# Attention and a multiplicative ffn on one core: the planner's choices replaced by written-out orders for five engines

## The chip, the cores and the metric

The kernel runs on one core of one Trainium2 chip. The metric is the device time of one execution in microseconds; the time of a kernel is the median of its runs. Profiles come from one profiled execution each; its span runs from the first to the last instruction of the program.

## What is computed

```python
# q, k, v: 8 batches, 12 heads, 448 positions, 64 per head; x: 3584 tokens, d_model 768, d_ff 1024
q_n, k_n = rmsnorm(q, g_q), rmsnorm(k, g_k)
scores = scale * np.matmul(q_n, k_n.transpose(0, 1, 3, 2))
attn = np.exp(scores - max); attn = attn / attn.sum(-1)
x = np.matmul(attn, v)            # heads side by side: (3584, 768)
a, b = x @ w1, x @ w2
out = ((a * b) @ w3) @ w_out      # float32
```

## The kernel before

The 96 heads are worked in 24 quads of four heads, three quads to a batch. For each quad, q and k are loaded (`load_qk`), squared on ACT, summed on DVE, scaled to bf16 by DVE, and transposed, by TensorE for the first five quads (`do_turn`, L1163) and by a DMA on SP's queue for the others. The scores of a quad are seven units of two PSUM banks each (`do_score`, L716), and ACT's exp of each unit (L738) writes P. A value block (`start_pv`, L803 and L782) multiplies P with v and with ones for one quad or for two; ACT forms the reciprocal of the sums by Ln and Exp (L825, L826) and DVE multiplies it into xT (L845).

The product w3 @ w_out is formed once: each of eight blocks of 128 rows of w3 is loaded, turned by TensorE (`do_w3_turn`, L1185), copied to w3T, and used by one "w" pair of eight positions on w_out's four chunks. Then each batch has eight "f" pairs (`ffn1_pair`: for each two blocks of d_ff one with w1, whose sums are copied to a_sb by ACT or DVE, and one with w2, whose sums DVE multiplies with that copy into abT, L989), and each two batches have seven "o" pairs (`ffn2_pair`) that multiply abT with w34s and whose sums are copied to `half` (L369 on ACT, L375 on DVE) and stored. The last o tile is done apart (`do_last`, L1104).

A pair (`Pair`, `do_pass`, L908) has two PSUM banks. A pass is four matmuls on 64 by 64 tiles of TensorE, of 448 columns for f and 384 for w and o; f has 12 passes, w and o have 16. In the middle of a pair the two row halves change banks: `hand_over` puts an empty instruction on SP or POOL that waits for the last matmul of the first half, and the first matmul of the second half waits for it. Until `gap_at` no pass of the pair is planned.

All instructions are emitted by a `Planner` that runs its own clock over five engines with a duration for each job. Before the change, each of ACT, DVE, SP and POOL took, whenever it was free, the job that could start first, then the one with the lowest key; jobs with two possible engines went to the one that finished earlier; and TensorE's next step came from rules in `pe_try` with margins, limits and keys (`PAIRS`, `MARGINS`, `HUNGERS`, `STOCKS`, `AGAINST` and others). Whatever the planner chose is a fixed program on the chip: each engine runs its list in order and waits on semaphores. Weights, v and five of the quads' q and k are loaded through POOL's queue in the order of `POOL_ORDER`, at most eight transfers in flight; the others through SP's. Until 13.2 us of the planner's clock, TensorE fills free time with matmuls on a constant tile (`do_warm`, L1233), after sixteen longer ones at the start (L1360).

Of the kernel before, what the change touches and what calls it, by code (L numbers as in the profile page):

```python
# [23 lines left out]
DRAIN = 0.11  # L24
LAG = {"ACT": 0.11, "DVE": 0.09, "SP": 0.0, "POOL": 0.0}
# [3 lines left out]
BUSY = 75.0  # L29


class Job:
# [4 lines left out]
    def __init__(self, engine, took, key, emit, needs=(), done=None, moves=None):  # L37
        self.took = took if isinstance(took, dict) else {engine: took}
        self.key, self.emit, self.needs, self.done = key, emit, needs, done
        self.moves, self.any = moves, isinstance(took, dict)  # L40
# [5 lines left out]
class Planner:  # L46
# [3 lines left out]
    def __init__(self):  # L50
        self.free = {e: 0.0 for e in ("ACT", "DVE", "SP", "POOL", "PE")}
        self.jobs = []
# [5 lines left out]
    def add(self, *args, **kw):  # L58
        self.jobs.append(Job(*args, **kw))
# [37 lines left out]
    def commit(self, job, start, engine):  # L97
# [3 lines left out]
        self.jobs.remove(job)  # L101
# [28 lines left out]
    def run(self, pe_step, finished):  # L130

        stuck = 0
        while not finished() or self.jobs:
            best = None
            behind = {
                e: sum(
                    job.took[e]
                    for job in self.jobs
                    if e in job.took
                    and not job.any  # L140
                    and job.ready() <= max(self.free[e], self.now) + 0.3
                )
                for e in ("ACT", "DVE")
            }
            for e in ("ACT", "DVE", "SP", "POOL"):
                mine = []
                for job in self.jobs:
                    if e not in job.took:
                        continue
                    ready = job.ready()  # L150
                    if job.moves is not None:
                        ready = max(ready, self.lane_free(e))
                    if ready < INF:
                        at = max(ready, self.free[e], self.now)
                        if job.any and any(
                            max(ready, self.free[x], self.now) + job.took[x] + behind[x]
                            < at + job.took[e] + behind[e]
                            for x in job.took
                        ):
                            continue  # L160
                        mine.append((at, job.key, job))
                if not mine:
                    continue
                first = min(m[0] for m in mine)
                start, _, job = min(
                    (m for m in mine if m[0] <= first + 1e-9), key=lambda m: m[1]
                )
# [1285 lines left out]
```

## Time and profile before

| | |
|---|---|
| Median of 3 runs | 350.99 us (350.04 to 351.31) |
| Span of the profiled execution | 348.0 us |
| PE busy | 342.3 us, 98% |
| ACT, DVE, POOL busy | 260.8, 206.7, 76.9 us |
| Chain that ended last | PE 98%, of which L908 68%, L803 13%, L716 9% |
| Granted TensorE clock | 0.998 over the span |
| DMA | 55.11 MB, 158 GB/s on average |

The execution's own time is its span and some 3 us around it. PE busy is the union of the matmuls' own durations; since a matmul of 0.35 us is followed by the next pass after 0.19 us, a busy PE need not be a PE that starts a pass as soon as it can. For that the start of one pass is to be set against the start of the next. A letter q behind an engine's name (POOLq, SPq) is its queue of instructions that only issue or wait.

### The profile page before, as it was taken

Reading aid. Unit: us, or ns where it says so; the run is one execution under the profiler, and the core shown is the slowest. Engines: PE = TensorE matmul, PEld = TensorE weight load, DVE = VectorE, ACT = ScalarE, POOL = GpSimd, SP = SyncE. Lnnn points to the kernel's source line nnn. Section 1 sums busy time; section 2 is a strip of 40 time slices with the busy share of each in tenths; the row PEclk is TensorE's granted clock in tenths of the full one; section 3 lists DMA queues with packets and bytes.
Section 4 is the critical chain, followed back from the end, with each engine's and each line's share of the span. In section 5 each row is a group of like instructions: output and inputs, shape, how many; then the busy total and the mean of one; then the engine's idle time right before and its main releaser. Section 6 shows DMA issues by size and latency. Waiting matters only on the chain.

```text
span 348.0 us, 16174 instructions
## 1 busy us (share of the span) xinstructions
PE 342.3 (98%) x7373; PEld 219.3 (63%) x7373; DVE 206.7 (59%) x296; ACT 260.8 (75%) x371; POOL 76.9 (22%) x134
## 2 busy tenths in 40 slices
PE   8999999999999999999999999999999999999995
PEld 4767756656775756566666575566665665666674
DVE  5369289898956687486567963865894313222100
ACT  4779989999997997998799797978987882222122
POOL 8556820302222301222022022212204000000000
PEclk9999999999999999999999999999999999999999
DMA  8999999499995969948898699477898051000055
GB/s 197 206 312 204 241 299 268 89 202 199 208 187 174 92 156 188 260 107 154 148 246 161 169 165 259 116 131 186 197 185 105 7 133 53 4 2 2 4 166 155
DMA packets 68488, 55.11 MB, mean 158 GB/s; under 512 B 45060, under 2 KB 62372, under 8 KB 68420
## 3 DMA queue, kind: packets, MB, share of 16 engines
q1 hardware_dynamic: 49440, 35.33, 43.0%
q0 software_dynamic: 18048, 16.92, 29.6%
q10 hardware_dynamic: 932, 1.84, 1.4%
q8 instruction: 57, 0.93, 1.1%
q14 instruction: 11, 0.09, 0.1%
HBM read 46.66 MB, written 11.01 MB: 166 GB/s over the span
## 4 chain that ended last, share of the span: by engine, by line
PE 98%; ACT 1%; DVE 0%; issue 0%
PE ps_all L908 68%; PE ps_all L803 13%; PE ps_all L716 9%; PE ps_all L782 2%; PE ps_all L1360 2%; PE ps_all L1163 1%; PE ps_all L1185 1%; PE ps_all L1104 1%; PE ps_all L1233 1%; ACT P L738 0%; DVE abT L989 0%; ACT qk_sb L369 0%; DVE warm_t L1343 0%; PE ps_all L1373 0%
## 5 line engine op out<-in xcount | busy, mean ns | idle before, releaser
L738 ACT ACTIVATE P<-ps_all 128x896 bf16<-128x896 f32 x114 | 99.5, 916 | 11.7 <-PE ps_all L716 10.8
L424 POOL DMA_DIRECT2D v_sb<-in_v_dram x96 | 57.3, 611 | 184.1 <-PE ps_all L716 120.3
L908 PE MATMUL ps_all<-xT,w2s 64*64 64x448 bf16 x1536 | 88.5, 349 | 0.0
L908 PE MATMUL ps_all<-xT,w1s 64*64 64x448 bf16 x1536 | 86.5, 349 | 0.0
L908 PE MATMUL ps_all<-w34s,abT 64*64 64x384 bf16 x1728 | 80.2, 323 | 0.4 <-DVE abT L989 0.4
L369 ACT ACTIVATE half<-ps_all 128x896 bf16<-128x896 f32 (+1 forms) x35 | 30.6, 874 | 48.5 <-PE ps_all L908 48.3
L908 PEld LDWEIGHTS <-abT 64*64 64x64 bf16 x1728 | 51.7, 107 | 20.3 <-issue 0.7
L908 PEld LDWEIGHTS <-w2s 64*64 64x64 bf16 x1536 | 46.5, 107 | 25.6
L908 PEld LDWEIGHTS <-w1s 64*64 64x64 bf16 x1536 | 46.0, 107 | 25.7 <-issue 0.4
L716 PE MATMUL ps_all<-qkT 64*64 64x448 bf16 x672 | 60.3, 351 | 0.0
L989 DVE TENSOR_TENSOR abT<-ps_all,half 128x896 bf16<-128x896 f32 x32 | 34.8, 1089 | 41.2 <-PE ps_all L908 41.1
L492 DVE TENSOR_REDUCE ssq<-sq 128x14 f32<-128x896 f32 (+1 forms) x50 | 51.2, 1041 | 12.5 <-ACT sq L487 12.2
L526 DVE TENSOR_TENSOR qks<-qk_sb,al 128x448 bf16<-128x448 f32 x96 | 54.6, 616 | 4.8 <-ACT al L504 4.7
L487 ACT ACTIVATE sq<-qk_sb 128x896 f32<-128x896 f32 (+1 forms) x50 | 45.1, 917 | 1.6 <-DMA qk_sb<-in_q_dram 1.3
L845 DVE TENSOR_TENSOR xT<-ps_all,r 128x448 bf16<-128x448 f32 x48 | 27.5, 618 | 25.6 <-ACT r L826 22.0
L716 PEld LDWEIGHTS <-qkT 64*64 64x64 bf16 x672 | 21.7, 106 | 13.2 <-issue 4.2
L908 PE MATMUL ps_all<-w_outs,w3T 64*64 64x384 bf16 x512 | 25.1, 324 | 0.1
L803 PE MATMUL ps_all<-P,v_sb 128*32 128x448 bf16 x456 | 25.0, 352 | 0.0
L738 ACT ACTIVATE w_outs<-ps_all 128x896 bf16<-128x896 f32 x24 | 21.4, 915 | 3.2 <-PE ps_all L716 3.0
L803 PEld LDWEIGHTS <-v_sb 128*32 128x32 bf16 x592 | 15.9, 97 | 12.2 <-issue 0.2
L738 ACT ACTIVATE Pr<-ps_all 128x896 bf16<-128x896 f32 x24 | 22.1, 920 | 0.6 <-PE ps_all L716 0.5
L375 DVE COPY half<-ps_all 128x768 f32<-128x768 f32 x13 | 12.4, 955 | 12.7 <-PE ps_all L908 12.7
(63 smaller groups left out, 210.9 us busy)
## 6 DMA issues: line engine op xcount, KB each, us to landing
out_dram<-half SPq DMA_DIRECT2D x48, 192.0 KB, 3.3
qk_sb<-in_q_dram SPq DMA_DIRECT2D x15, 448.0 KB, 6.3
qk_sb<-in_k_dram SPq DMA_DIRECT2D x15, 448.0 KB, 5.4
v_sb<-in_v_dram POOLq DMA_DIRECT2D x48, 64.0 KB, 4.0
v_sb<-in_v_dram POOLq DMA_DIRECT2D x48, 48.0 KB, 4.1
qk_sb<-in_q_dram POOLq DMA_DIRECT2D x5, 448.0 KB, 8.7
qk_sb<-in_k_dram POOLq DMA_DIRECT2D x5, 448.0 KB, 9.4
w3s<-in_moe_w_dram POOLq DMA_DIRECT2D x8, 256.0 KB, 6.8
```

The source lines that it names most:

```text
L369: nc.scalar.activation(out=out, in_=in_, func=AF.Copy, scale=1.0 if by is None else by)
L375: nc.vector.tensor_copy(out=out, in_=in_)
L424: nc.gpsimd.dma_start(out=v_bufs[i % 4][p0 : p0 + HP, g::2, 0 : j1 - j0].rearrange("p h j d -> p h (j d)"), in_=src[:, g::2, j0:j1].rearra ...
L487: nc.scalar.activation(out=out, in_=in_, func=AF.Square)
L492: nc.vector.tensor_reduce(out=s["ssq"][:, t, x0:x1], in_=s["sq", t][:, x0:x1], axis=AX, op=ADD)
L526: nc.vector.tensor_tensor(out=s["qks"][:, t, :, x], in0=src[:, t, x], in1=s["alpha"][:, t, x].unsqueeze(2).broadcast_to([NP, NJ, D]), op=MULT,
L716: nc.tensor.matmul(out=sc[HP * c : HP * c + HP, u, 0:S].rearrange("p (j s) -> p j s", j=NJ), lhsT=qkT[u * D : (u + 1) * D, 1, j, cols], rh ...
L738: lambda: nc.scalar.activation(out=dst, in_=sc[:, :, 0:S], func=AF.Exp),
L803: nc.tensor.matmul(out=ps_all[hd * HALF : (hd + 1) * HALF, z, 0:S], lhsT=value_weights(i, hd, j, kind), rhs=s["P"][:, hd, j, :] if j < NF ...
L845: lambda: nc.vector.tensor_tensor(out=xT[b][:, 2 * m + kind - 1, :], in0=ps, in1=s["r"], op=MULT),
L908: mm = nc.tensor.matmul(out=ps_all[64 * h : 64 * h + 64, p.bank + z, 0 : p.n], lhsT=lhsT[64 * r : 64 * r + 64, 64 * h : 64 * h + 64], rhs= ...
L989: nc.vector.tensor_tensor(out=abT[bp][:, f0 : f0 + 2, odd * S : (odd + 1) * S], in0=ps_all[:, z : z + 2, 0:S], in1=a_sb[b, f0], op=MULT,)
```

## The change

Five strings list what each engine does, in order: `PE_ORDER` (x: turn of a w3 block, t: turn of a quad's q or k, s: score unit, V and v: value block and its steps, w, f, o: passes of the pair with that number, L: last tile), `ACT_ORDER` and `DVE_ORDER` (s squares, r sums, a scales, c scaled q and k, T, x, w, f, o copies, e exps, n reciprocals, m and h products, g gains), `SP_ORDER` and `POOL_ORDER` (l, v, W loads, t transposes, O, Z stores, hand-overs not listed). The planner keeps its clock and takes the next name of each list as soon as its conditions hold; `follow` replaces `pe_try`. On POOL two blocks of w3 (`Ww0 Ww1`) now stand ahead of w_out's first chunk, and q and k of quad 1 ahead of its last; TensorE turns the two blocks first. `gap_at` lies 0.32 us behind the hand-over instead of 0.15; banks that have been free for `WHILE` = 0.3 us are preferred; constants of the planner's clock change. A job that fills a buffer of `half` now has its condition at the copy (`free_of`) and no longer at the pair's start.

```diff
+WHILE = 0.3
...
+PE_ORDER = (
+    "x0 x1 t*2 w0 s w0 s x2 s w0*2 w1*2 s w0*2 w1*2 s w1*2 w0 s w0 w1*2 w0 w1*2 s w2 w0 w2*3 w0 "
+    "w1 V1 v*2 w2*2 w0 w2*4 w1 w0 w1 w0 w2*2 w1 w0*2 w2 w1 w2 w1 x3 x4 t w2 w3*3 w4 w3*2 w4 w3*2 "
...
+    "f12*3 s f13*6 V2 v*8 f14 s f14*5 f15 s f15*2 f14 s f15 f14 f15 f14 s f15 f14 s f14*2 f15 s "
+    "f15*5 s*4 o3*6 o4*5 o3*2 o4*3 s o3*3 s o3*4 o4 o3 s o4*7 V2 v*8 s o5*5 o6 o5 o6 s o6 o5*2 o6 "
...
+ACT_ORDER = (
+    "s0q0 s0q1 s0k0 s0k1 a0q a0k T0q e0.0 e0.1 e0.2 e0.3 e0.4 e0.5 e0.6 n0 s1q0 s1k0 a1q w0 w1 "
...
+DVE_ORDER = (
+    "r0q0 r0q1 r0k0 r0k1 c0q0 gp c0q1 c0k0 c0k1 gs x0 T0k x1 x2 m0.1 m0.2 r1q0 r1k0 c1q0 c1q1 x3 "
...
+POOL_ORDER = (
+    "Ww0 Ww1 Wo0 Ww2 Wo1 Wo2 v0.3 v0.2 v0.1 v0.0 l1q0 l1k0 Wo3 Ww3 Ww4 l2q0 l2k0 Ww5 l3k0 Ww6 "
...
+    "v6.2 v8.2 v8.0 v6.3 v8.1 v9.0 v9.2 v9.3 v9.1 v10.1 v8.3 v11.1 v10.2 v10.0 v10.3 v11.0 v12.1 "
...
+    "v18.0 v19.1 v20.3 v18.3 v20.2 v21.3 v23.0 v20.0 v21.0 v20.1 v22.1 v21.1 v21.2 v23.2 v22.0 "
...
+                if self.done[e] == len(ORDERS[e]):
                     continue
...
+                job = self.jobs.get(ORDERS[e][self.done[e]])
+                if job is None:
+                    continue
+                ready = job.ready()
+                if job.moves is not None:
+                    ready = max(ready, self.lane_free(e))
+                at = max(ready, self.free[e], self.now)
+                if at < INF and (best is None or at < best[0]):
+                    best = (at, job, e)
...
-    POOL_ORDER = (
-        "o0 w0 w1 w2 o1 o2 v0 u0 o3 q1 w3 w4 q2 w5 v1 u1 a0 w6 w7 v2 u2 a1 u3 v3 q3 a2 b0 b1 q4 q5 b2".split()
-    )
...
-    FIRST = 3.5
+    FIRST = 2.9
...
-        p.gap_at = free[e] + 0.15
+        p.gap_at = free[e] + 0.32
...
+    def follow(t, step):
+        early, idle = idle_banks(t - WHILE), idle_banks(t)
+        idle = early + sorted((z for z in idle if z not in early), key=lambda z: bank_at[z])
+        two = adjacent(early)
+        two = adjacent(idle) if two is None else two
+        one = single(early or idle)
+        kind = step[0]
+        if kind == "s":
+            n = next_score[0]
+            i, g = divmod(n, NU)
+            if two is None or max(qkT_at[i]) + SEM > t:
+                return None
...
+            return do_score(t, two)
...
+        p = next((p for p in pairs if p.id == step), None)
+        if p is None:
+            p = next((p for p in waiting if p.id == step), None)
+            if p is None or two is None or p.ready() > t:
+                return None
+            waiting.remove(p)
+            start_pair(p, two)
+            return do_pass(p, t)
+        return do_pass(p, t) if p.ready() <= t else None
...
+    def pe_step(t):
+        if place[0] >= len(ORDER):
             return None
...
+        took = follow(t, ORDER[place[0]])
+        if took is not None:
+            place[0] += 1
+        elif t < WARM_TO and idle_banks(t):
             return do_warm(single(idle_banks(t)))
         return took
...
-            warm(1)
+            free["PE"] = max(free["PE"], plan.now + 0.35)
...
-        warm(WARM)
+        warm(WARM + 1)
```

## Rows read from the trace of the kernel before

**Rows 1.** The page, busy us (share of the span) and instructions of each engine

```profile
PE 342.3 (98%) x7373; PEld 219.3 (63%) x7373; DVE 206.7 (59%) x296; ACT 260.8 (75%) x371; POOL 76.9 (22%) x134
```

**Rows 2.** Waits of PE: who waited for whom, us in total, times, longest

```profile
PE ps_all L908 <- DVE abT L989: 0.4, 1, 0.4
```

**Rows 3.** The chain that ended last, in order of time: start us, us, what

```profile
18.16 2.46 PE ps_all L803 x48
...
168.22 3.41 PE ps_all L908 x84
...
215.48 0.69 PE ps_all L782 x24
216.17 3.52 PE ps_all L803 x72
...
222.46 2.27 PE ps_all L908 x48
...
289.29 52.05 PE ps_all L908 x1152
341.34 2.78 PE ps_all L1104 x64
```

**Rows 4.** Timeline, head: start, us, engine, line, out<-in, count [idle before <- releaser]

```profile
7.80 0.60 POOL L424 DMA_DIRECT2D v_sb<-in_v_dram  x1 [0.41 <-DMA w_outs<-in_moe_w_out_dram]
...
8.69 0.93 PE L1233 MATMUL ps_all<-warm_t 128*128 128x256 bf16 x7
...
9.10 0.59 POOL L424 DMA_DIRECT2D v_sb<-in_v_dram  x1 [0.70 <-DMA w3s<-in_moe_w_dram]
...
10.29 0.38 PE L1233 MATMUL ps_all<-warm_t 128*128 128x256 bf16 x2
...
11.05 0.57 PE L716 MATMUL ps_all<-qkT 64*64 64x448 bf16 x8
...
11.48 5.10 ACT L738 ACTIVATE P<-ps_all 128x896 bf16<-128x896 f32 x6 [1.59 <-PE ps_all L716]
...
12.80 0.97 PE L908 MATMUL ps_all<-w_outs,w3T 64*64 64x384 bf16 x12
...
13.56 0.73 POOL L384 DMA_DIRECT2D qk_sb<-in_k_dram  x1 [1.13 <-DMA w_outs<-in_moe_w_out_dram]
```

**Rows 5.** Timeline around the turns of w3 blocks 3 and 4

```profile
21.33 0.59 POOL L424 DMA_DIRECT2D v_sb<-in_v_dram  x1 [0.52 <-DMA qk_sb<-in_k_dram]
...
22.42 0.59 POOL L424 DMA_DIRECT2D v_sb<-in_v_dram  x1 [0.50 <-DMA w3s<-in_moe_w_dram]
...
23.92 1.32 PE L1185 MATMUL ps_all<-ident,w3s 128*128 128x128 bf16 x16
24.44 0.57 POOL L455 DMA_DIRECT2D w1s<-in_moe_w_dram  x1 [1.43 <-DMA w3s<-in_moe_w_dram]
24.47 0.60 PEld L1185 LDWEIGHTS <-w3s 128*128 128x128 bf16 x10 [0.21 <-issue]
```

**Rows 6.** Timeline at the end of batch 1, around 115 us

```profile
114.44 0.96 PE L716 MATMUL ps_all<-qkT 64*64 64x448 bf16 x12
114.67 1.09 DVE L989 TENSOR_TENSOR abT<-ps_all,half 128x896 bf16<-128x896 f32 x1 [0.23 <-PE ps_all L908]
...
115.81 1.33 PE L908 MATMUL ps_all<-w34s,abT 64*64 64x384 bf16 x28 [0.41 <-DVE abT L989]
```

**Rows 7.** Windows: stretch, then busy us (count) of PE, PEld, DVE, ACT, POOL; clock, DMA, GB/s

```profile
5.00:15.00 10.00, 9.88 (x141) 7.17 (x143) 6.86 (x14) 6.64 (x13) 5.77 (x9) 1.00 1.15 203
45.00:100.00 55.00, 55.00 (x1176) 35.76 (x1164) 48.16 (x70) 50.69 (x79) 11.32 (x20) 1.00 0.91 207
```

**Rows 8.** DVE's copies of f sums, forms kept apart: busy us, mean ns | idle before

```profile
L375 DVE CAST half<-ps_all 128x896 bf16<-128x896 f32 x11 | 12.0, 1090 | 11.1 <-PE ps_all L908 10.9
```

**Rows 9.** Timeline of PE's weight loads in the fill of the start

```profile
4.58 0.15 PEld L1360 LDWEIGHTS <-warm_t 128*128 128x128 bf16 x1 [0.28 <-issue]
5.01 0.15 PEld L1360 LDWEIGHTS <-warm_t 128*128 128x128 bf16 x1 [0.28 <-issue]
```

More of the change, by code (lines that the diff above doesn't have):

```diff
@@ L29, with unfold @@
 BUSY = 75.0
+PE_ORDER = (
[41 rows of a table added]
+)
+ACT_ORDER = (
[18 rows of a table added]
+)
+DVE_ORDER = (
[18 rows of a table added]
+)
+SP_ORDER = (
[9 rows of a table added]
+)
+POOL_ORDER = (
[8 rows of a table added]
+)
+def unfold(text):
+    return [
+        x.split("*")[0] for x in text.split() for _ in range(int((x + "*1").split("*")[1]))
+    ]
+ORDER = unfold(PE_ORDER)
+ORDERS = {
+    "ACT": ACT_ORDER.split(), "DVE": DVE_ORDER.split(),
+    "SP": SP_ORDER.split(), "POOL": POOL_ORDER.split(),
+}
 class Job:
@@ L100, in commit @@
         end += LAG[engine]
-        self.jobs.remove(job)
+        del self.jobs[ORDERS[engine][self.done[engine]]]
+        self.done[engine] += 1
         job.at = start
@@ L134, in run @@
             best = None
[L135 to L141, printed above, removed]
-                )
-                for e in ("ACT", "DVE")
-            }
-            for e in ("ACT", "DVE", "SP", "POOL"):
[L146 to L162, printed above, removed]
-                    continue
[L164 to L167, printed above, removed]
-                if best is None or start < best[0]:
-                    best = (start, job, e)
+            for e in ("ACT", "DVE", "SP", "POOL"):
+                if self.done[e] == len(ORDERS[e]):
+                    continue
+                job = self.jobs.get(ORDERS[e][self.done[e]])
[7 more added lines that the diff above has]
+                    best = (at, job, e)
             pe_at = max(self.free["PE"], self.now)
@@ L830, in done @@
                 s["r_at"] = e + SEM
-            add("ACT", 1.06, -1000.0, reciprocal, needs=[lambda: at], done=done)
+            add("n%d" % i, "ACT", 1.05, -1000.0, reciprocal, needs=[lambda: at, lambda: all_of(m_at[i - 2], 2) if i >= 2 else 0.0], done=done)
             return
@@ L861 @@
     running = [None]
+    made = {}
     class Pair:
@@ L1201, in do_w3_turn @@
         return took
-    def next_pair(t):
-        if len(pairs) >= (EARLY_PAIRS if w_at["w_out"][3] == INF else PAIRS[phase()]):
-            return None
-        return next((p for p in waiting if p.ready() <= t), None)
-    def any_turn(t, r, idle, n):
-        if not idle:
-            return None
-        if turns:
-            i, w = turns[0]
-            if scaled_at[i][w] <= r:
-                turns.pop(0)
-                return do_turn(t, i, w, single(idle))
-        ready = [fc for fc in w3_turns if w_at["w3"][fc] + SEM <= r]
-        if ready and (len(ready) >= n or ready[-1] == CF - 1):
-            if ready[0] - len(w34_at) < AHEAD_W3:
-                return do_w3_turn(t, w3_turns.pop(0), single(idle))
-        return None
@@ L1399, with weight @@
         seq = [0]
-        def weight(emit, moves, done):
-            add("POOL", 0.6, -100.0 + seq[0], emit, done=done, moves=moves)
-        for name in POOL_ORDER:
+        def weight(name, emit, moves, done):
+            add("W" + name, "POOL", 0.6, -100.0 + seq[0], emit, done=done, moves=moves)
+        for name in LOADS.split():
             what, x = name[0], int(name[1])
```

281 lines of the change are left out of this document (119 added, 162 removed), and 85 rows, old and new, of tables (ACT_ORDER, DVE_ORDER, PE_ORDER, POOL_ORDER).

## The prediction

> **What bounds the kernel now.** I read the busy row of the page first, then PE's waits, then the chain of work that ended last. PE is busy for 342.3 of 348.0 us [rows 1], and in the whole run its longest wait inside the work is one of 0.4 us, for a product of DVE [rows 2]. That leaves two questions: does a busy PE work at its rate, and how much of its time is not work. The chain answers the first. Twelve passes of 448 columns take 2.27 us (0.189 us each), 21 passes of 384 columns 3.41 us (0.1624 us each), and a double value block 0.69 + 3.52 = 4.21 us. The last 288 passes, with nothing but ffn work, take 52.05 us; 192 x 0.189 + 96 x 0.1624 = 51.9 us [rows 3]. So PE runs at its rate, at the full clock, and the work itself cannot shrink: the change removes no pass.
>
> Now the sum of the work, with the counts of the lists, which are those of the old kernel too: 768 f passes and 168 score units at 0.189 us (145.2 + 31.8), 432 o and 128 w passes at 0.1624 (70.2 + 20.8), eleven double value blocks at 4.21 (46.3), two single ones at 2.46 (4.9) [rows 3], 18 turn groups of about 0.42 (7.6), and the last tile 2.8 [rows 3]. Together 329.6 us. From the first turn (the warm-up fill that follows it starts at 8.69 [rows 4], 0.4 us after it) to the end of the last tile at 344.1 [rows 3] are some 335.7 us. So only about 6 us between them are no work. Of these, PE's changes between kinds of work (ffn passes, turns, value sums) take most: I count 54 such changes in the old order and 54 in the new list, kind for kind, so they stay. What order can win is the rest: 0.93 + 0.38 us of warm-up fill between the first turns, 0.29 us in the w passes at 12.80 (twelve matmuls in 0.97 us, where three passes span 0.68) [rows 4], 0.26 us in the turns of w3 blocks 3 and 4 (the two groups would span 1.06, two at 0.45 and 0.16 for the last matmul's own end, and span 1.32) [rows 5], and 0.8 us at 115 [rows 6]. That is 2.7 us, 0.8%. Anything over that must come from nowhere in this trace.
>
> **Head: blocks 0 and 1 of w3 ahead of w_out.** The POOL queue's waits show its landings, since an issue waits for the one eight places before: w_out chunk 0 by 7.80, w3 block 0 by 9.10, w_out chunk 1 by 13.56 [rows 4]. A block takes 1.3 us, a chunk 1.9. Put first, block 0 lands 1.9 - 1.3 = 0.6 us before chunk 0 did, at about 6.9 to 7.2, block 1 at 8.2 to 8.5, chunk 0 at 10.2 to 10.4. The list makes PE turn both blocks before the first turn of q, so that turn goes from 8.3 to about 8.8; its copy is ACT's and has room, since the first scores wait for the copy of k, which needs the second turn and has its place on DVE behind one w3 copy: it is done at about 10.7 in both kernels. First scores then at about 10.85 instead of 11.05 [rows 4]. The seven exps that follow (0.84 us apart, six in 5.10 us with the last one's own 0.92) end about 0.2 us earlier, and the first value block can start at about 17.5 instead of 18.1 [rows 3]. But the new list has 26 w passes ahead of it, the old order 28: 0.6 - 0.32 = some 0.27 us won. That is 0.27 of the 1.6 us that the head loses; the rest stays lost because PE is then held by ACT's exps and by w_out's chunks, and no longer fills.
>
> After that block both orders do 20 w passes and then blocks 3 and 4. The two loads of quad 1 now go ahead of w_out's chunk 3; the bytes are the same, so chunk 3 lands where k's load landed before, by 21.33 [rows 5]. The list needs it after eight w passes: 17.5 + 2.4 + 0.1 + 8 x 0.1624 = 21.3, just in time (0 to 0.2 us lost). Block 4 is the gate. In the old order its turn was not late for its load: the stop lies inside the turn of block 3, after six of its eight weight loads, and the profile puts it down to issue; block 4 had landed by 24.44 [rows 5], less the 0.3 us that an issue trails a landing. The new list comes to it earlier: value block done at 20.0, 20 w passes, block 3 from 23.4, block 4 wanted at 23.8. If it lands as before, at some 24.2, PE waits 0.4 us, turns it at 24.3 instead of 24.6 and has two w passes (0.32) less behind it: even. If the stop of 0.26 in block 3's turn comes again on top: +0.26. If block 4 lands a block's 1.3 us after block 3 (by 22.42), so before 23.8: -0.4. I take 0.0, from the row of the same bytes, and keep both ends. The Trainium skill (DMA: Bandwidth & Descriptors, the section on queues, rings and completion order) says that each of the sixteen engines takes its own ring in order, while the engines finish one transfer independently of each other; a strict queue would give the -0.4, rings drifting apart the 0.0, and the rows with block 4 two microseconds behind block 3 speak for the second.
>
> **The stop at 115.** At the end of batch 1 nothing is left for PE but three scores and an o pair that reads the product of the f pair just finished. DVE starts that product 0.23 us after the pair and takes 1.09 us; the o pair starts at 115.81, 1.56 us after the pair's last pass began (114.25, one pass before the score that shows at 114.44) [rows 6]. The new list has the same place: five f15 passes, four scores, then o3. The chain of 1.56 us stays; scores and the pass fill 0.189 x 5 = 0.945 us of it instead of 0.756. So the idle time falls from 0.80 to 0.61 us, if the fourth score finds banks; the banks of four scores in a row come free at ACT's 0.81 to 0.84 us each, so it may come too late and win little. Between -0.19 and 0: I take -0.1.
>
> **Hand-overs and banks.** A half pair's hand-over counts 0.32 us after its empty instruction instead of 0.15, so other passes are put between the halves; this costs nothing while other pairs are open (the new list mixes f and o passes, both with 64-row tiles, a change that costs nothing in the chain: f to o at 0.189, o to f at 0.162). Banks free for 0.3 us are preferred. In the profiled run hand-overs cost almost nothing, so the gain there is 0; but the three runs lie between 350.04 and 351.31, and late hand-overs are one cause that such a spread can have. I credit a third of the 0.95 us from median to lowest: -0.3, bounds 0 to -0.95.
>
> **Small edits.** The fill matmul that stood behind the product of the gains now stands with the others ahead of it; PE fills there anyway, so 0 (without that cover, one matmul of 0.2 us). The planner's new constants move its own clock alone: with the orders listed they still choose banks, fill and the engine of a hand-over, and cost nothing of themselves.
>
> **Copies moved.** Of the 24 f copies before the last two batches, ACT has 8 in the lists, before 13; DVE gets five more at 1.09 us, ACT loses five at 0.92, the exp's own size and time [rows 4, 8]. None is on the path that sets the end as long as DVE keeps up: from 45 to 100 it is busy for 48.16 of 55 us [rows 7] and gets about two there, 50.3 of 55. Cost 0, cover 4.7 us; what a loss of that cover costs is the second rival. Orders of SP and POOL: POOL's list puts some v pieces behind loads that wait for a later quad's buffer (v6.3 behind v8.2 and v8.0, v20.0 behind v23.0), and hand-over instructions stand in the same queues; each has several microseconds before its value block reads it. Cost 0 to +0.8, one more stop of the size at 115; I take 0.
>
> **Sum.** 0.0 - 0.1 - 0.3 + 0 = -0.4 us on the median of 350.99 (the profiled span is 348.0; some 3.0 us lie outside it and stay): **350.6 us**. The bounds add up to -0.4 - 0.19 - 0.95 = -1.5 and +0.26 + 0.2 + 0.8 = +1.3: 349.5 to 352.3. About 0.5%, or 1.75 us, is what a measurement of this kernel can tell from no change; the forecast lies inside.
>
> **Rivals.** First, everything order can win is won: no stop at 115, no wait about block 4, the head filled. For it: PE is the only bound and the loss is known place by place. Against: the list itself keeps f15, scores, o3 and keeps block 4 right behind block 3. 350.99 - 2.7 = 348.3, with one place left 348.8. Chance 0.15. Second, DVE becomes the bound: from 45 to 115 it gets f copies and keeps all products. For it: 92% busy with them by the sum above. It decides once DVE runs more than a product (1.09 us) late, since a pair's two banks then stay closed and PE stops as at 115, 0.6 to 0.8 us each; with four such places 2.4 to 3.2 us: 353.8. Against: the old trace has one wait of PE for DVE, at 115, and DVE was idle before that product [rows 2, 6]. Chance 0.09. Third, the clock. The rows show 1.00 for the granted clock from 5 to 15 us [rows 7], with turns between warm-up fill; weights for the 512-column fill were loaded 0.43 us apart at 4.58 and 5.01 [rows 9], at 1.2 GHz, where fill of 256 columns later took 0.11 each. If the clock fell as fill gives way to turns, a stretch like the first, 1.2 to 5.3 us, would run at half speed: 2.05 us lost, 353.0. Chance 0.03. The Trainium skill (TensorE: Matmul & The Clock Gate, Part 4 on transposes) says that transposes do not count as activity for the gate; by that rule the new head, with two more turn groups before the scores and less fill, is the place to look. Fourth, the lists turn out to give nearly the old timing everywhere: 351.0, chance 0.04. The forecast has the other 0.69.
>
> **How the numbers follow.** Faster by over 0.5% (below 349.24): the first rival and 0.01 of the forecast's edge, 0.16. Slower (above 352.74): second and third rival and 0.01, 0.13. The rest, 0.71. For 8 in 10 the range goes from 349.0, which takes in part of the first rival, to 352.4.
>
> **What would show it.** Right: first scores near 10.85, first value block near 17.5, the turn of block 4 near 24.3; three or four scores and then an idle PE of 0.6 us near 113 to 115, released by the product; 54 changes of kind; last tile ending 0 to 1 us earlier. Wrong: PE waiting on banks held by DVE between 60 and 110, a granted clock below 1.00 after 7 us, more than one wait over 0.3 us after 25 us, or no stop at all before o3.

## The result: 1.4% slower, and where the time went

The changed kernel takes 355.82 us (median of 4, 355.21 to 355.91) beside 351.15 us of the kernel before: a ratio of 1.0141, 95% interval 1.0113 to 1.0168, so 4.0 to 5.9 us more. The forecast was 350.6 us with a range of 349.0 to 352.4; the measured time lies above it. Every ratio, and the medians of E6 and E8, leave out slow executions (one each of E6 and E8). The profiled run took 355.91 us, its span is 354.1 us at a granted clock of 0.996, 6.1 us over the span of the kernel before.

This pair of profiles overstates the loss. In every execution for which both are on record the time is 1.73 to 1.86 us over the span; the "some 3 us around it" named ahead of the prediction came from setting a median beside the span of one execution. So the profiled execution of the kernel before stands for some 349.8 us, 1.3 us under its median, and the one of the changed kernel for its median.

The page of the changed kernel, busy row and the row of TensorE's code queue (packets, MB, share of the DMA engines):

```profile
PE 346.3 (98%) x7368; PEld 240.3 (68%) x7368; DVE 218.0 (62%) x307; ACT 252.1 (71%) x360; POOL 76.8 (22%) x134
...
q8 instruction: 57, 0.93, 1.1%
```

Beside [rows 1], PE is again busy for 98%: the busy row hides the loss, since a stop of 50 ns between pipelined matmuls doesn't show as idle. PEld rises from 219.3 to 240.3 us though it loads the same weights, at 107 ns for each of the passes' loads in both pages: fewer of them overlap. That doesn't measure the loss, for E7, which loses less than half as much, still has 238.7 us. DVE has its 11 us more and ACT its 9 us less, as the lists say.

The chain of the changed kernel (start us, us, what), its head, its last stretch and the last tile:

```profile
9.40 0.62 PE ps_all L1261 x8
10.02 0.39 PE ps_all L1239 x7
...
18.99 2.46 PE ps_all L871 x48
...
293.43 52.75 PE ps_all L981 x1152
346.17 2.78 PE ps_all L1180 x64
```

The single value block takes 2.46 us and the last tile 2.78 us, to the hundredth what [rows 3] shows. The last 288 ffn passes, the very same work, take 52.75 us instead of 52.05: 0.70 us of stops in a stretch where no load and no score is left. That is the pattern of the whole kernel. To see it everywhere I added up the work of the passes done (0.189, 0.1624 us and so on, as in the forecast) and compared the times at which both kernels had done the same amount ("lag" is the difference):

```
work done (us)   before at   changed at   lag    what lies between
     7             16.9        18.0       1.16   head: turns, first scores, first w_out passes
    30             41.2        42.3       1.03   turns of blocks 3 and 4 win 0.25
    34             45.3        47.6       2.27   43 to 46 us: +1.24
    95            107.7       110.1       2.43
   105            118.6       121.2       2.59   stop at the end of batch 1
   150            164.2       167.2       3.07
   210            224.9       228.5       3.55
   270            285.5       289.6       4.14
   328            343.9       348.8       4.84   from 118 us on: +2.3, in steps under 0.15
  end of span     348.0       354.1       6.1    tail: +1.27
```

**The head.** The timeline of the changed kernel (columns as in [rows 4]):

```profile
7.46 0.62 PE L1261 MATMUL ps_all<-ident,w3s 128*128 128x128 bf16 x8
...
9.40 0.62 PE L1261 MATMUL ps_all<-ident,w3s 128*128 128x128 bf16 x8 [0.45 <-DMA w3s<-in_moe_w_dram]
9.64 0.59 POOL L517 DMA_DIRECT2D v_sb<-in_v_dram  x1 [1.34 <-DMA w3s<-in_moe_w_dram]
...
11.52 0.73 POOL L477 DMA_DIRECT2D qk_sb<-in_q_dram  x1 [1.29 <-DMA w_outs<-in_moe_w_out_dram]
...
11.89 0.38 PE L801 MATMUL ps_all<-qkT 64*64 64x448 bf16 x4
```

PE stands before the turn of block 1 until 9.40, because the list wants that turn before the two turns of q and k, and block 1 lands at 9.35 (POOL's issue follows at 9.64); chunk 0 of w_out lands at 11.24. The first scores come at 11.89 instead of 11.05 [rows 4].

The clock in that stretch (columns as in [rows 7]):

```profile
5.00:15.00 10.00, 9.54 (x112) 5.57 (x114) 6.83 (x14) 5.57 (x11) 5.35 (x9) 1.00 1.13 198
```

**43 to 46 us.** PE's timeline, and the waits of its weight loads from 43 to 46 us (who for whom: us in total, times, longest):

```profile
42.91 0.83 PE L981 MATMUL ps_all<-w_outs,w3T 64*64 64x384 bf16 x14
44.14 0.51 PE L981 MATMUL ps_all<-w_outs,w3T 64*64 64x384 bf16 x6 [0.40 <-issue]
```

```profile
PEld L981 <- issue: 0.8, 1, 0.8
PEld L981 <- SPq L965: 0.5, 1, 0.5
```

The first is a hole of 0.59 us in the middle of a pass, with no semaphore to wait for; the second is the hand-over of pair w7 (line 965), whose two halves the list puts next to each other: 0.41 us between passes that need none. The value block behind them waits another 0.13 us longer than before for the last exp.

**From 118 us on.** Waits of PE's weight loads from 118 to 346 us, first the changed kernel, then the kernel before:

```profile
PEld L801 <- issue: 3.3, 11, 0.8
PEld L981 <- issue: 3.2, 14, 0.4
PEld L871 <- issue: 3.0, 8, 0.4
PEld L850 <- issue: 2.6, 8, 0.4
```

```profile
PEld L803 <- issue: 3.0, 8, 0.4
PEld L782 <- issue: 2.6, 8, 0.4
PEld L716 <- issue: 2.6, 7, 0.4
PEld L908 <- issue: 0.4, 1, 0.4
```

Passes (L981, before L908) were held up noticeably once and are now held up 14 times, scores (L801, before L716) 11 times instead of 7; value blocks are the same. The starts of passes and scores show it more sharply. Behind 118 us, 29 of them come over 30 ns later than the spacing of 0.189 or 0.1624 us asks for, each 41 to 43 ns after the release of a PSUM bank by an exp, a copy or a product (22 by ACT, 7 by DVE). One is the stop at the end of batch 1 below; the other 28 are 43 to 136 ns late and make 2.1 us together, of the 2.3 us of lag gathered there. Eight of them, 0.70 us, lie in the last 288 passes and are the whole difference between 52.75 and 52.05 us. In the kernel before there is not one such start behind 118 us.

**End of batch 1** (beside [rows 6]):

```profile
117.00 0.87 PE L801 MATMUL ps_all<-qkT 64*64 64x448 bf16 x12
117.25 1.09 DVE L1065 TENSOR_TENSOR abT<-ps_all,half 128x896 bf16<-128x896 f32 x1 [0.31 <-PE ps_all L981]
...
118.40 0.38 PE L801 MATMUL ps_all<-qkT 64*64 64x448 bf16 x4 [0.53 <-ACT P L823]
118.59 0.68 PE L981 MATMUL ps_all<-w34s,abT 64*64 64x384 bf16 x12
```

The o pair no longer waits for the product; the fourth score in front of it waits for ACT to free its banks, and the two holes there (0.11 and 0.73 us) sum to what the one was.

**The tail.** SP's queue at the end (DMA issues), kernel before, then changed:

```profile
342.39 0.47 SPq L1045 DMA_DIRECT2D out_dram<-half  x1
343.29 1.67 SPq L1119 DMA_DIRECT2D out_dram<-qk_sb  x2
```

```profile
347.26 2.07 SPq L1121 DMA_DIRECT2D out_dram<-half  x3
349.43 1.61 SPq L1195 DMA_DIRECT2D out_dram<-qk_sb  x2
```

SP's list ends `O3.2.0 O3.5.0 O3.4.0 O3.3.0 Z0.0 Z1.0`. The copy for O3.5.0 ends at 347.24; those for O3.3.0 and O3.4.0 had ended at 345.3 and 346.7, but their stores stand behind it. Three stores of 0.5 to 0.9 us then run in a row, and the two of the last tile behind them.

### The profile page after: what moved, and what is told of

It reads as the page before. It is cut to its first block, busy times and chain, and to the rows that moved or that the text cites. A ratio compares the mean times of both kernels' runs of the same rounds, so it can differ in the third digit from the quotient of the medians.

```text
span 354.1 us, 16139 instructions
## 1 busy us (share of the span) xinstructions
PE 346.3 (98%) x7368; PEld 240.3 (68%) x7368; DVE 218.0 (62%) x307; ACT 252.1 (71%) x360; POOL 76.8 (22%) x134
## 4 chain that ended last, share of the span: by engine, by line
PE 94%; DMA 2%; ACT 2%; POOL 1%; issue 0%; DVE 0%; POOLq 0%; SPq 0%; ACTq 0%
PE ps_all L981 67%; PE ps_all L871 12%; PE ps_all L801 9%; PE ps_all L850 2%; DMA w3s<-in_moe_w_dram 2%; PE ps_all L1239 1%; ACT w_outs L823 1%; PE ps_all L1261 1%; PE ps_all L1180 1%; PE ps_all L1348 0%; POOL v_sb L1419 0%; ACT P L823 0%; ACT Pr L823 0%; POOL w3s L554 0%; DVE qk_sb L468 0%
## 5 line engine op out<-in xcount | busy, mean ns | idle before, releaser
L981 PE MATMUL ps_all<-xT,w2s 64*64 64x448 bf16 x1536 | 104.0, 350 | 0.0
L981 PE MATMUL ps_all<-xT,w1s 64*64 64x448 bf16 x1536 | 101.8, 350 | 0.0
L981 PE MATMUL ps_all<-w34s,abT 64*64 64x384 bf16 x1728 | 83.9, 323 | 0.0
L981 PEld LDWEIGHTS <-abT 64*64 64x64 bf16 x1728 | 59.4, 107 | 13.1 <-issue 0.7
L981 PEld LDWEIGHTS <-w2s 64*64 64x64 bf16 x1536 | 53.5, 107 | 18.8 <-issue 0.8
L981 PEld LDWEIGHTS <-w1s 64*64 64x64 bf16 x1536 | 51.6, 107 | 21.4 <-issue 2.5
L801 PE MATMUL ps_all<-qkT 64*64 64x448 bf16 x672 | 62.0, 353 | 0.5 <-ACT P L823 0.5
L462 ACT ACTIVATE half<-ps_all 128x896 bf16<-128x896 f32 (+1 forms) x26 | 22.4, 862 | 47.8 <-PE ps_all L981 47.8
L801 PEld LDWEIGHTS <-qkT 64*64 64x64 bf16 x672 | 26.3, 106 | 13.2 <-issue 4.0
L468 DVE CAST half<-ps_all 128x896 bf16<-128x896 f32 x19 | 20.7, 1090 | 17.3 <-PE ps_all L981 17.3
L981 PE MATMUL ps_all<-w_outs,w3T 64*64 64x384 bf16 x512 | 26.0, 325 | 0.5 <-issue 0.4
```

The costliest lines, as they stand in the source:

```text
L462: nc.scalar.activation(out=out, in_=in_, func=AF.Copy, scale=1.0 if by is None else by)
L468: nc.vector.tensor_copy(out=out, in_=in_)
L801: nc.tensor.matmul(out=sc[HP * c : HP * c + HP, u, 0:S].rearrange("p (j s) -> p j s", j=NJ), lhsT=qkT[u * D : (u + 1) * D, 1, j, cols], rh ...
L981: mm = nc.tensor.matmul(out=ps_all[64 * h : 64 * h + 64, p.bank + z, 0 : p.n], lhsT=lhsT[64 * r : 64 * r + 64, 64 * h : 64 * h + 64], rhs= ...
```

## The experiments

Times are medians; every ratio is against the kernel before on the same chip, with its 95% interval, and is not the quotient of the two medians. The changed kernel stands at 1.0141 (1.0113 to 1.0168). E1 to E4 were timed together; E4 (355.73 us), whose lists are those of the changed kernel, can stand for it among them.

### E1: the order of the last stores

```diff
-    "O3.2.0 O3.5.0 O3.4.0 O3.3.0 Z0.0 Z1.0"
+    "O3.2.0 O3.3.0 O3.4.0 O3.5.0 Z0.0 Z1.0"
```

> The changed kernel with two entries of SyncE's list put back in the order in which their copies end: the store O3.5.0 goes from before O3.4.0 and O3.3.0 to behind them. Nothing else differs. Theory (the list is carried out as written, so a store whose copy ends at 347.24 us holds back two stores that were ready at 345.3 and 346.8, and the last two stores of all are issued behind that row): the last store is issued some 0.8 us earlier, and the time from the last matmul to the last landing shrinks from 4.4 us to 3.1 to 3.6 us, so the kernel gains 0.8 to 1.3 us, about 354.5 to 355.0 us. Rival (the stores are bound by the data's own way to memory, or by the copy of the last tile): the last landing moves by less than 0.2 us and the time stays at 355.8.

354.90 us, ratio 1.0098 (1.0074 to 1.0123). SP's queue:

```profile
346.25 1.12 SPq L1121 DMA_DIRECT2D out_dram<-half  x2
348.04 1.58 SPq L1195 DMA_DIRECT2D out_dram<-qk_sb  x2
```

The stores no longer queue up. From the end of the last matmul to the end of the span it is 4.6 us, against 5.2 to 5.3 in the changed kernel, E2, E3 and E4 and 3.9 in the kernel before. The other runs agree: 4.5 to 4.7 us in E6, E7 and E9, which have this order of stores, 5.8 and 6.0 in E8 and E5, which have not. So the trace gives the store order 0.6 us, beside 0.9 us between the medians and a forecast of 0.8 to 1.3; the head of this execution was also 0.35 us earlier, with the same code. The mechanism is as expected, the size in the trace somewhat under it. Of the tail's 1.27 us some 0.7 stay unexplained: the last issue comes 0.7 instead of 0.4 us after the last matmul, and takes 2.8 instead of 2.5 us to land.

### E2: the head as before

```diff
-    "x0 x1 t*2 w0 s w0 s x2 s w0*2 ...
+    "t*2 x0 x1 s*2 w0*2 x2 s w0*2 ...
-    ... gs x0 T0k x1 x2 ...      (VectorE)
+    ... gs T0k x0 x1 x2 ...
-    "Ww0 Ww1 Wo0 Ww2 ...         (POOL)
+    "Wo0 Ww0 Ww1 Ww2 ...
```

> The changed kernel with the head put back: chunk 0 of w_out is loaded ahead of blocks 0 and 1 of w3 again, the two qk turns stand ahead of the block turns on TensorE, and VectorE copies in that order. Everything behind the first 13 us is as in the changed kernel. Theory (the new load order costs about 1 us at the head, because chunk 0 lands at 11.24 us in place of 7.52, and the turn of block 1 at TensorE's head waits for a landing at 9.35 us): the first value block starts at 17.9 to 18.2 us in place of 18.92, and the time falls by 0.8 to 1.1 us to about 354.8. Rival (the head's loss is made up again at the turns of blocks 3 and 4 near 24 us, or by the scores' exps at 46 us, which are late anyway): under 0.3 us.

356.39 us, ratio 1.0147 (1.0122 to 1.0172): no gain. The first value block did start at 18.09 as expected, but in the profiled run 0.4 us were lost inside that block and 0.3 us each at 31 and 43 us to the kind of hole that E5 is about, and 0.8 us at 147 us to a v load that landed late:

```profile
PEld L850 <- DMA v_sb<-in_v_dram: 0.8, 1, 0.8
```

The other runs show why the head is worth less than the pair of profiles says. The first load on POOL's queue lands anywhere from 6.68 to 8.68 us (on average at 7.46 where it is a block of w3, at 7.91 where it is chunk 0), and the whole head moves with it. First value block, by kernel: 18.92, 18.57, 18.77, 18.36, 19.27, 18.04, 18.54 with the new head (changed kernel, E1, E3 to E6, E8; mean 18.64); 18.09, 18.14, 18.84 with the old head and the same lists behind it (E2, E7, E9; mean 18.36); 18.09, 18.73, 18.70 in the kernel before, B2 and B3, with two w_out passes (0.32 us) more ahead (mean 18.51, on equal work 18.19). The new head thus costs 0.3 to 0.45 us on average; the rest of the 1.1 us was that one pair of executions, and is part of the 1.3 us by which the profile of the kernel before lies under its median.

### E3: a pass of margin at 19 places

```diff
-... f2*2 s f0 f3*2 f2*2 f3 s ... f14*2 f15 s f15*5 s*4 ...
+... f2*2 s f0 f2 f3*2 f2 f3 s ... f14*2 f15*2 s f15*4 s*4 ...   (19 such places behind 58 us)
```

> The changed kernel with 19 places of TensorE's list changed behind 58 us: where a score or the first pass of a new pair waited 40 to 130 ns for a PSUM bank, one pass of an open pair (ready by then) is put ahead of it, so that the bank has 0.19 us more to come free. Theory (the list starts such work in the very moment in which its bank comes free, with no margin): most of these 19 stops, together about 1.6 us with the drains they bring, go, and the time falls by 0.8 to 1.5 us to 354.3 to 355.0. Rival (the copies and exps that free the banks are themselves the pace, so that a start that is put back puts back the next release too): the stops reappear one or two items later, and the time stays within 0.4 us of 355.8.

354.33 us, ratio 1.0093 (1.0069 to 1.0117), 1.5 us under the changed kernel by the medians, 1.7 by the ratios and 1.4 under E4. The chain's last stretch and the weight loads' waits from 118 to 346 us:

```profile
293.04 52.17 PE ps_all L981 x1152
```

```profile
PEld L801 <- issue: 2.7, 7, 0.7
...
PEld L981 <- issue: 1.6, 5, 0.4
PEld L981 <- POOLq L965: 0.7, 3, 0.4
```

The last 288 passes are back to within 0.12 us of [rows 3], the held-up passes fall from 14 to 5, the 28 short late starts behind 118 us to 10 (0.7 us), and the lag gathered from 60 us to the last matmul falls from 2.4 to 1.25 us. E1, E2, E4, E5 and E8, which keep the order of passes, have 27 to 31 of them (2.1 to 2.3 us), so they belong to the order and not to one execution. The theory of the missing margin holds; the moved passes bring three hand-over waits of their own.

### E4: the constants of slack as before

```diff
-WHILE = 0.3
+WHILE = 0.0
-        p.gap_at = free[e] + 0.32
+        p.gap_at = free[e] + 0.15
```

> The changed kernel with the two constants of slack as before: a pair's second half may be planned 0.15 us after its hand-over in place of 0.32, and a PSUM bank needs no 0.3 us of planned idleness to be preferred. The order of every engine is the same list, so only the choice of banks differs, and with it which release a start waits for. Theory (the lists set the pace and the banks all come free just in time, whichever is taken): within 0.5 us of 355.8, the small stops stay. Rival (the preference for longer idle banks is what makes or saves the stops): if it saves them, the small stops behind 60 us grow by over 1 us, 357 or more; if it makes them, the time falls below 355.

355.73 us, ratio 1.0123 (1.0099 to 1.0147), last stretch 52.74 us. With the order fixed by lists, the preference for idle banks and the wider hand-over change nothing: the stops come from the order. The hole at 43 us is larger here (0.79 us shown as idle):

```profile
45.01 0.51 PE L981 MATMUL ps_all<-w_outs,w3T 64*64 64x384 bf16 x6 [0.79 <-issue]
```

### E5: the hole in the w6 pass, and TensorE's code

```diff
-            for _ in range(n):
+            for size in [512] * (n - 6) + [96] * 30:
-                    out=ps_all[:, 7, :], ... rhs=warm_t,
+                    out=ps_all[:, 7, 0:size], ... rhs=warm_t[:, 0:size],
```

> The changed kernel with 48 more instructions on TensorE at its very start: the last 6 of the 16 warm-up matmuls of 512 columns are replaced by 30 of 96 columns, which fill the same idle time ahead of the first turn. All lists are the same. In the changed kernel and in the three runs with the same lists and E2, TensorE stops inside a w6 pass near 43.4 us for 0.33 to 0.99 us with no semaphore to wait for, always ahead of its 1473rd recorded instruction; the only other stops without a wait stand ahead of instructions 449, 705 and 961, all of which are one more than a multiple of 256 away from each other or exactly that. Theory (TensorE's code comes in pieces of 16 KB, 256 instructions, over a DMA queue of its own, and the piece comes late while the loads keep the DMA engines busy): the stop is tied to the count, so it leaves its w6 pass and stands 48 instructions, 6 passes, earlier in the work, near 42.2 to 42.6 us, again ahead of recorded instruction 1473. Rival (something in that w6 pass, its operands or its bank): it stays at the same pass. The time is within 1 us of 355.8 either way.

357.13 us, ratio 1.0159 (1.0122 to 1.0196). PE's timeline over the same w6 passes:

```profile
42.29 0.84 PE L981 MATMUL ps_all<-w_outs,w3T 64*64 64x384 bf16 x16
42.94 0.38 PE L801 MATMUL ps_all<-qkT 64*64 64x448 bf16 x4
43.13 1.00 PE L981 MATMUL ps_all<-w_outs,w3T 64*64 64x384 bf16 x20
```

The hole has left its pass, so it isn't that pass's operands or bank. It did not come back 48 instructions earlier either: here the piece of code arrived in time (its fetch began 2.74 us after the piece before was used up, and 2.78 us before it was needed). What ties the hole to the code is the count: in all profiles the holes without a semaphore stand ahead of recorded instructions 449, 705, 961, 1473, 1729 and, in B3, 6593, all 193 more than a multiple of 256; and queue 8 brings 57 packets of 16 KB for some 14,740 instructions, one for each 256. The records of that queue give the rest:

```
                          fetch begins after the        first instruction after   hole
                          piece before is used up (us)  the fetch begins (us)     (us)
before, instr. 1473             0.55                          4.81                none
changed, 1473                   3.61                          2.46                0.59
E1, 1473                        3.78                          2.28                0.57
E2, 1473                        3.42                          2.40                0.33
E3, 1473                        3.97                          2.32                0.79
E4, 1473                        4.17                          2.30                0.99
E5, 1473                        2.74                          2.78                none
all runs, behind 65 us      -1.1 to 4.4                   mostly over 4           rarely
```

Where PE stopped, the first instruction came 2.2 to 2.6 us after the start of its packet. Up to 57 us, while the loads fill the DMA engines (a DMA share over 1.0 in the windows under E8), the packet mostly starts 2.1 to 4.5 us late; 256 instructions of w_out passes last some 5.4 to 6 us, so PE stops where the sum of the two is larger (3.61 + 2.46 = 6.07 us in the changed kernel, whose piece lasts 5.48 without the hole). In the kernel before that fetch happened to start early. But no time was won by moving the hole, this run's head being late (first load at 8.39 us) and its tail 0.8 us longer, so its price is taken from the traces alone: 0.3 to 1.0 us.

### E6 and E7: the mends together

E6 is E1, E3 and an edit at 43 us; E7 adds E2's head.

```diff
-... w6*2 s w7 w6*4 s w7*4 V2 v*8 ...
+... w6*2 s w7 s w7*2 w6*4 w7*2 V2 v*8 ...
```

> The changed kernel with the store order of E1, the 19 shifted starts of E3, and one more edit: at 43 us the last score of batch 0's first pair goes ahead of the last four w6 passes, and these four stand between the first half's end of pair w7 and its second half. Theory (three independent losses add): the two earlier gains of 1.3 and 1.7 us, and 0.4 to 0.7 us at 45 us (the 0.41 us wait for the hand-over of w7 and the 0.2 us wait of the value block for the last exp go), together 3.2 to 3.7 us, 352.1 to 352.6 us, a ratio to the kernel before of 1.002 to 1.005. Rival (the gains are the same time counted twice, since each of them only moves the wait to the next release): 353.8 or more.

> The kernel of E6 with the head of E2 (chunk 0 of w_out loaded first, qk turns first). Theory (the head's load order costs 0.8 us to the first value block, and what E2 lost again were stops for code and one late load of v that don't belong to the head): 0.4 to 0.8 us less than E6, 351.4 to 352.2 us, about the kernel before. Rival (the head's 0.8 us is taken back by the fetch of code, which comes late whenever TensorE is early while the DMA engines are full): within 0.3 us of E6, or slower.

E6: 354.15 us, ratio 1.0080 (1.0055 to 1.0104): by its median the rival's. E7: 352.97 us, 1.0059 (1.0035 to 1.0083): under E6 as the theory has it, over the forecast range. The store order and the margins add up only in part. The edit at 43 us won nothing: the hand-over's wait is gone, but the earlier score waits 0.28 us for banks, and the value block now waits for the copy of w6's sums, which the edit had put back (E6's timeline):

```profile
45.43 0.38 PE L850 MATMUL ps_all<-Pr,v_sb 64*32 64x448 bf16 x8 [0.22 <-DVE w34s L468]
```

### E8: half of w1 and w2

```diff
-            out=dst[:, 2 * m : 2 * m + 2, :]...  in_=src...[m],
+            out=dst[:, 2 * m : 2 * m + 1, :]...  in_=src...[m][:, 0:DFF],
-            wt[:, c, (f0 + x) * 128 : ...
+            wt[:, c - c % 2, (f0 + x) * 128 : ...
```

> The changed kernel with half of w1 and w2 left out: each of their six loads brings one of its two row groups, and the matmuls take the loaded group in the place of the other, so that the DMA engines move some 1.5 MB less between 33 and 60 us, and every list and every instruction of TensorE is as it was. What it computes is therefore not the reference's. Theory (TensorE's code is late because its fetch stands behind the loads on busy DMA engines): the fetches for instructions 1473 and 1729, which begin 3.4 to 4.2 us after the piece before them is used up in the changed kernel, begin under 2 us after it, the first instruction of the piece is reached with over 3 us to spare, the stop without a wait in the w6 pass near 43.4 us goes (0.53 us of it), and the time is 0.4 to 1.0 us less, 354.8 to 355.4. Rival (the delay of a fetch is set by something other than the loads): the fetch begins 3.4 to 4.2 us late as before and the stop stays at 0.3 to 1.0 us.

355.94 us, ratio 1.0119 (1.0082 to 1.0155): the time expected didn't come. Windows (columns as in [rows 7]; last three: clock, DMA share, GB/s), changed kernel, then E8:

```profile
38.00:44.00 6.00, 5.74 (x138) 4.11 (x131) 2.75 (x4) 6.00 (x8) 1.79 (x4) 1.00 1.04 216
44.00:57.00 13.00, 12.77 (x260) 7.46 (x263) 9.61 (x14) 8.95 (x20) 1.47 (x3) 1.00 1.07 274
```

```profile
38.00:44.00 6.00, 6.00 (x144) 4.38 (x136) 2.46 (x4) 5.63 (x7) 2.95 (x5) 1.00 1.09 252
44.00:57.00 13.00, 12.91 (x268) 7.54 (x266) 9.85 (x15) 9.72 (x19) 0.74 (x2) 1.00 0.65 157
```

The other loads moved up into the room, so the engines stayed full up to 50 us (a share of 1.00 from 47 to 50, 0.25 from 50 to 54): the fetch for instruction 1473 began 3.42 us late and the one for 1729 3.2 us (3.55 in the changed kernel), neither under the 2 us that I expected, and a hole of about 0.2 us stayed. The next fetch, at 50.8 us, where the share had fallen, began 1.05 us late instead of 3.26. That speaks for the loads as the cause of the delay, but from one fetch; it is not shown for the hole itself.

### E9: a second pass of mending

```diff
-... f27 f26 f27 s f27 ... o18 s o20 ...
+... f27 f26 f27*2 s ... o18 o20 s ...        (11 such places; w7 in one piece)
```

> The kernel of E7 with a second pass of the same mending: 11 more starts of a score or pair behind 50 us that waited 48 to 212 ns for a bank in E7's trace get one pass of another pair ahead of them, and the last score of batch 0's first pair is put two passes later than in E7, with pair w7 in one piece again. Theory (what is left behind 60 us is again a start without margin): 0.5 to 0.9 us less than E7, 352.1 to 352.5. Rival (at this point each mended start puts back the next release, and the rest of the loss is in the drains between kinds of work): within 0.3 us of E7, 352.7 to 353.3.

353.69 us, ratio 1.0066 (1.0040 to 1.0091): the rival's, no gain over E7. Of the eight late starts that E7 has between 50 and 118 us three are left, but behind 118 us there are 12 short ones instead of 10, and the last stretch is the same 52.17 us. In the profiled run, the longest of eight, two new stops show, one on a hand-over at 265 us (0.5) and one on a late v load:

```profile
148.03 0.56 PE L851 MATMUL ps_all<-Pr,v_sb 64*32 64x448 bf16 x13 [0.66 <-DMA v_sb<-in_v_dram]
```

In the changed kernel the same load had landed 1.1 us before that value block began. So no version made from these lists beat the kernel before.

### B1 to B3: parts of the change on the kernel before

B1 takes the load order alone, B2 the hand-over's slack alone, B3 takes the kernel's margin for banks away.

```diff
-        "o0 w0 w1 w2 o1 o2 v0 u0 o3 q1 w3 ...       (B1)
+        "w0 w1 o0 w2 o1 o2 v0 u0 q1 o3 w3 ...
-        p.gap_at = free[e] + 0.15                    (B2)
+        p.gap_at = free[e] + 0.32
-    MARGINS = (0.267, 0.281)                         (B3)
+    MARGINS = (0.0, 0.0)
```

> The kernel before with one part of the change alone: its list of POOL's loads begins w0 w1 o0 (blocks 0 and 1 of w3 ahead of chunk 0 of w_out), and q1 stands ahead of o3. TensorE's order is still found by its own rules, and so can turn to what has landed. Theory (the new load order costs the head about 1 us: chunk 0 lands some 3.7 us later and the first w_out passes with it): the first scores and w_out passes move, the first value block starts 0.3 to 1.1 us later than 18.09, and the time rises by 0.3 to 1.1 us. Rival (it was the list's order of turns and copies, not the loads, that cost the head): within 0.2 us of the kernel before.

> The kernel before with the hand-over's slack of the change alone: a pair's second half may be planned 0.32 us after the hand-over in place of 0.15. The orders of the other four engines come out the same, TensorE's differ in 181 lines, a few passes that change places. Theory (the slack has nothing to win, since the hand-overs of the kernel before show no wait in its trace): within 0.5 us of the kernel before. Rival (any small change to the rules' input turns a tuned order into an ordinary one, as the load order alone did for 3 us): 1 to 4 us slower.

> The kernel before with its margin for banks taken away: its rules first look for work whose PSUM banks have been idle for 0.267 or 0.281 us and only then for any; here they take any at once. The rules then find another order on all engines. Theory (starting work in the moment in which its bank comes free costs a stop each time, as in the changed kernel): small stops of 40 to 130 ns ahead of scores and pair starts appear by the dozen behind 60 us, and the time rises by 1 to 3 us, 352 to 354. Rival (the margin does nothing, the stops of the changed kernel come from its banks or its lists): within 0.5 us of the kernel before.

B1: 354.68 us, ratio 1.0091 (1.0057 to 1.0126), 3 us where I expected up to 1.1. The head itself is late by 0.5 us in the profile; the rest is that the rules, starting from there, find another order on all engines, with stops of its own, only two of them short late starts behind 118 us (PE's timeline):

```profile
118.26 1.50 PE L908 MATMUL ps_all<-w34s,abT 64*64 64x384 bf16 x32 [1.27 <-DVE abT L989]
```

B2: 350.82 us, 0.9990 (0.9965 to 1.0014): nothing, and not every small edit costs. B2 has no late start behind 118 us either. B3: 359.02 us, 1.0211 (1.0181 to 1.0240), 7.4 us where I expected 1 to 3. Waits of its weight loads from 118 to 346 us:

```profile
PEld L716 <- issue: 4.6, 15, 0.4
PEld L908 <- issue: 3.9, 12, 0.8
...
PEld L908 <- POOLq L892: 2.0, 3, 0.9
```

Passes held up 12 times instead of once, scores 15 times instead of 7, and 25 late starts behind 118 us, 4.7 us together, where the kernel before has none: the picture of the changed kernel, from taking its margin. Since the rules also reorder everything else, not all of the 2.1% is the margin's.

## The prediction, point by point

- **The sum of the work** held: PE worked at its rate, value blocks and the last tile took the same hundredths. But the step drawn from it failed, and it is the one that made the forecast wrong. That order can win no more than 2.7 us bounds the gain; it says nothing of the loss. I had no term for stops that the new order makes where the old one had none, and these are most of the result: 28 late starts of 2.1 us behind 118 us, 1.2 us at 43 to 46 us, 0.6 us of stores in the wrong order.
- **The 3.0 us outside the span** are 1.8 us; the sum doesn't use them.
- **The clock**, the third rival, stayed at 1.00 in the row from 5 to 15 us. I had read two turn groups more into the new head; both heads have four ahead of the first scores and five up to 15 us, and only the fill is less (17 matmuls of 256 columns instead of 22). By the rule of the Trainium skill (TensorE: Matmul & The Clock Gate, Part 4) it was the place to look, and no fall shows.
- **Head, 0.27 won** (in the sum it ends in block 4's 0.0): wrong in sign, 0.3 to 0.45 us lost on average and 1.1 in the profile. The landing of block 1 (8.2 to 8.5 forecast, 8.35 to 9.63 over seven runs) and of chunk 0 (10.2 to 10.4, in fact 10.22 to 11.48) were the best cases, worked out from differences of landings; and the list makes the turns of q and k wait behind block 1, where the rules had filled.
- **Block 4, 0.0**: near in size, but not for the reason given. Block 4 was no gate: it had landed at 24.19 us, and the two turns began at 24.76, in one piece of 1.07 us instead of 1.32. The old stop of 0.26 us was TensorE's code: it stands ahead of recorded instruction 705, whose fetch had begun 3.9 us after the piece before was used up; in B2 the same turn stops at the same count, for 0.48 us.
- **The stop at 115, -0.1**: 0.0. The doubt I named decided: the fourth score's banks came too late.
- **Hand-overs and banks, -0.3**: the term that failed worst. The slack itself is worth 0 (E4, B2), and the spread of the runs had no such cause. I read the preference for idle banks as slack that the change adds. The old rules already had more: they first looked for work whose banks had been idle, and whose operands had been ready, for 0.27 us. Written down as a list, that margin is gone wherever the list does not keep it, and the order starts work at the moment of release: +2.3 us from 118 us on, of which E3 gave back 1.2 in the trace.
- **Pair w7**: not in the sum. The list puts its halves next to each other ahead of a value block: 0.41 us, which the same paragraph should have looked for.
- **Copies on DVE, 0**: right; inside the work no wait of PE for DVE over 0.3 us is left, and the rival of a DVE bound did not occur.
- **SP and POOL, 0 (to +0.8)**: I read POOL's list for v pieces, and in some runs one was 0.7 to 0.8 us late as the bound allowed (E2, E9). I did not read the end of SP's list: one store ahead of two that were ready, 0.6 us in a tail of +1.27.
- **Not foreseen at all**: the code fetch, 0.3 to 1.0 us at 43 us.
- **What would show it wrong** named the right kind of stop at the wrong place: PE did come to wait on banks, but mostly from 118 us on and not between 60 and 110, and held by ACT's exps more than by DVE. Its third sign, more than one wait over 0.3 us behind 25 us, did appear (0.59 and 0.41 at 43 to 46 us, 0.73 at 118). Of the signs of being right, the first scores (11.89 for 10.85), the first value block (18.92 for 17.5) and the end of the last tile (4.8 us later) all came out late.

Added up: head 0.4, 43 to 46 us 1.2 (code 0.59, hand-over 0.41, last exp 0.13), margins 2.3, tail 1.3: 5.2 us, beside a measured 4.0 to 5.9.

## What to carry to other kernels

An order that is written out must keep the slack that the rules had: look for each start in the list that comes at the very moment its bank or operand is released, and put one ready pass ahead of it (E3 won some 1.4 us so, a second round in E9 nothing); the busy row will not show what it costs, the duration of the same passes in the chain will. When a whole schedule is exchanged, what it can win is bounded by the idle time one sees, but what it can lose is not, so the range belongs mostly on the slow side; and every queue's list is read to its last entry, since stores issue in order.

## What the hardware showed

- TensorE's instructions came in pieces of 16 KB, 256 instructions, on a DMA queue of their own (57 packets for 14,736). Up to 57 us, with the DMA engines full, a fetch mostly began 2.1 to 4.5 us after the piece before it was used up, and where the engine stopped at the border it was for 0.1 to 1.0 us, with nothing but "issue" in the rows, and 2.2 to 2.6 us after the packet's start.
- The first 256 KB or 384 KB load on POOL's queue landed between 6.68 and 8.68 us in fourteen profiled runs; heads of the same code differed by up to 1.2 us.
- PE started 41 to 43 ns after the release of the bank that it waited for, in 29 starts of the changed kernel; 28 of these were 43 to 136 ns late, with PE at 98% busy.
